# Separate buffers for the last results of W2, and a written order for VectorE and ScalarE, in a float32 chain of attention and two feed-forward layers

## The chip, the cores and the metric

The kernel runs on one core of a Trainium2 chip. Its time is the device time of one execution: 863.34 us is the median of three runs (862.12 to 864.36). One more execution was recorded by the profiler; it took 863.14 us, and its recorded span, from the first to the last instruction, is 861.4 us. Times inside the trace count from the start of that span. PE is TensorE, DVE VectorE, ACT ScalarE, POOL GpSimd, and SP SyncE, which issues most DMAs.

## The reference

```python
# attention: 4 x 8 heads, 768 positions in chunks of 32, window 16 + 32 + 8, 8 memory keys
scores = scale * matmul(q_c, k_full.T); a = softmax(scores); out[c] = matmul(a, v_full)
x = out.transpose(0, 2, 1, 3).reshape(3072, 512)
# first layer, d_ff 1024
h = x @ w_in;  solu = h * softmax(h)
ln = (solu - mean(solu)) / sqrt(var(solu) + 1e-6) * g_ln
x = ln @ w_out
# second layer, d_ff 2048
h = x @ w_in2; g = maximum(0.01 * h, h); out = g @ w_out2
```

Weights come as float64 and are decoded on the chip; everything is computed to float32 accuracy.

## The kernel before, in words

W1, W2, W3 and W4 are the four weight matrices. A float32 product is made from two halves of each operand, a high half (a rounded copy, made by ACT) and a low half (the rest, made by DVE with a subtraction), and three matmuls: high by high, high by low, low by high. A "split" below is one such ACT copy and one such DVE subtraction.

*First stage.* 24 tiles of 128 tokens go through attention, W1, the softmax-like function and the normalization (`s_h`, line 274), a transposition (`s_lt`, 305), and W2 (`s_o`, 343). W2's result for one block of 512 tokens and one quarter `ec` of the 512 features is one accumulator `x2p` of 128 x 512; it takes 24 matmuls, three for each of 8 slices of 128. Two accumulators of PSUM take turns. Each finished one is copied by ACT to the buffer `x2s` (line 356) and stored to `x2d` in HBM by a DMA that ACT issues (line 357). `x2s` has one buffer (`bufs=1`), so a copy must wait until the store of the copy before it has landed. There are 24 such results; the last four, those of block 5, are computed in a loop of their own after the last token tile (line 555).

*Second stage.* W3 is applied to `x2` in a scheme with 7 products instead of 8 on 2 x 2 blocks (P1 to P7). Its operands are sums of quarters of `x2`: `x_steps` (line 504) forms four sums on DVE (lines 510, 512, 516, 526) and splits seven operands (`split`, lines 506 to 508: ACT line 507, DVE line 508), one `yield` after each step. The token blocks make three sets: blocks 0 and 1 (`xs0`, from tile `xt` into the tiles `xP1` to `xP7`), blocks 2 and 3 (`xs1`, from `xtq` into `L2`, `L3` and `xm`), and blocks 4 and 5 (later, into `xP1` to `xP7` again). W3's weights come in pieces, here `L0` and `L1`; `w3_steps` (line 542) splits one in two parts. A unit is one piece of weights by one set of tokens: 7 products of six matmuls each into three accumulators A, B and C (`w3_product`). Units 0 and 1 use `L0` with sets 0 and 1, units 2 and 3 use `L1`, and so on up to 24 units. Within a unit the products P1, P5, P6, P2 and P7 run first, P4 and P3 run during the next unit. After P1 the partial sum in C is copied to `s1`, and after P6 to `u2` (`keep`, line 682); the next product into C must wait for that copy.

*Order.* In the first stage a scheduler orders each engine. From line 535 SP's order is the written one, and from line 658 that of all engines is. Each slot of a unit ends with one or two background steps (`bg`, line 815): first the rest of `xs1`, then the split of `L1`, then the decoding of W4 (`w4_steps`), whose pieces are needed only after the 16th unit. Each engine executes its own instructions in order; one that waits holds up those behind it.

Of the kernel before, what the change touches and what calls it, by code (L numbers as in the profile page):

```python
# [9 lines left out]
F32 = mybir.dt.float32  # L10
F32R = mybir.dt.float32r
U32 = mybir.dt.uint32
AF = mybir.ActivationFunctionType
# [10 lines left out]
LAG = 5  # L24
# [15 lines left out]
def tile_kernel(  # L40
# [12 lines left out]
    nc = tc.nc  # L53
    P = 128
    NTILE = qt.shape[0]
# [5 lines left out]
    KD = DM // P  # L61
    KF = DFF // P
    KF2 = DFF2 // P
    BT = 512
    NBLK = NT // BT
    TB = BT // P
# [5 lines left out]
    x2d = dram.tile([NBLK, P, KD, BT], F32, name="x2d")  # L72
# [72 lines left out]
    sa, sh, satt, sps, sx2 = (ExitStack() for _ in range(5))  # L145
# [194 lines left out]

    open_x2 = {}

    def s_o(b, ec, lh, ll, part):
        if part == 0:
            open_x2[ec] = ps_x2.tile([P, BT], F32, name="x2p")
        ps = open_x2[ec]
        es = slice(ec * P, (ec + 1) * P)
        for kk in range(4 * part, 4 * part + 4):
            for n, (a, r) in enumerate(((w2h, lh), (w2h, ll), (w2l, lh))):
                nc.tensor.matmul(  # L350
                    ps, a[:, kk, es], r[:, kk],
                    start=(kk == 0 and n == 0), stop=(kk == KF - 1 and n == 2),
                )
        if part == 1:
            s = lp.tile([P, BT], F32, name="x2s", bufs=1)
            nc.scalar.activation(s, ps, AF.Copy)  # L356
            nc.scalar.dma_start(out=x2d[b, :, ec, :], in_=s)

    def att_steps(i, ld):
        sc, nms = s_scores(i, ld[0], ld[1])  # L360
# [21 lines left out]
    for d in LOADS:  # L382
# [3 lines left out]
        n = int(d[1])  # L386
# [17 lines left out]
    ENG = mybir.EngineType  # L404
# [5 lines left out]
    lp = sh.enter_context(tc.tile_pool(name="lp", bufs=2, reuse_waits="tile"))  # L410
    lb = {}
# [20 lines left out]
    for i in range(NTILE + 1):  # L432
        a = i + 2
        b, t = divmod(i, TB)
# [4 lines left out]
        if att:  # L439
            p, rs = s_exp(*s_scores(a, ld[0], ld[1]))  # L440
# [13 lines left out]
        if so is not None:  # L454
            j = i - 1
            s_lt(so, j // TB, j % TB, *lb[j // TB])
        so = nso
        if att:
            x = s_pv(pt, ld[2], rs)
# [6 lines left out]
        if 0 <= i - W3_FROM < KF2:  # L466
            f = i - W3_FROM
# [18 lines left out]
    PROD = ("P1", "P5", "P6", "P2", "P7", "P3", "P4")  # L486
# [5 lines left out]
    regr = sr.enter_context(tc.tile_pool(name="regr", bufs=1, side="right", reuse_waits="tile"))  # L492
    reg = {n: regr.tile([P, 4096], F32R, name=n) for n in ("L0", "L1")}
    xrp = sxr.enter_context(tc.tile_pool(name="xrp", bufs=1, side="right", reuse_waits="tile"))
    xr = {r: xrp.tile([P, 2, 2, BT], F32R, name=f"x{r}") for r in PROD}
    xtp = sxt.enter_context(tc.tile_pool(name="xtp", bufs=1, side="right", reuse_waits="tile"))

    def load_xt(v, tb):
# [5 lines left out]
    def x_steps(t, x):  # L504

        def split(r, src):
            nc.scalar.activation(x[r][:, 0], src, AF.Copy)
            tt(out=x[r][:, 1], in0=src, in1=x[r][:, 0].bitcast(F32), op=ALU.subtract)

        tt(out=t["b12"], in0=t["b22"], in1=t["b12"], op=ALU.subtract)  # L510
        yield
        tt(out=t["t2"], in0=t["b12"], in1=t["b11"], op=ALU.add)
        yield
        split("P1", t["b11"])
        yield
        tt(out=t["b11"], in0=t["b22"], in1=t["t2"], op=ALU.subtract)
        yield
        split("P5", t["b11"])
        yield
        split("P6", t["t2"])  # L520
        yield
        split("P2", t["b21"])
        yield
        split("P7", t["b12"])
        yield
        tt(out=t["b12"], in0=t["b21"], in1=t["t2"], op=ALU.subtract)
        yield
        split("P4", t["b12"])
        yield
        split("P3", t["b22"])  # L530
        yield

    ENGS = {ENG.PE, ENG.DVE, ENG.Activation, ENG.Pool, ENG.SP}
    order_ctx = ExitStack()
    order_ctx.enter_context(tc.manual_schedule(engines={ENG.SP}))
    def load_w3(q, n):
        nc.sync.dma_start(
            out=reg[n][:, 1792:3584].bitcast(F32), in_=w3f[q].rearrange("p r f -> p (r f)")
# [3 lines left out]
    def w3_steps(slot):  # L542
        for a, b in ((0, 1024), (1024, 1792)):
            h, l = slot[:, a:b], slot[:, 1792 + a : 1792 + b]
            nc.scalar.activation(h, l.bitcast(F32), AF.Copy)
            tt(out=l, in0=l.bitcast(F32), in1=h.bitcast(F32), op=ALU.subtract)
            yield

    def run(steps):
        for _ in steps:  # L550
            pass

    w3l = [load_w3(q, f"L{q}") for q in range(2)]
    xs0 = x_steps(load_xt(0, xtp.tile([P, 10, BT], F32, name="xt")), xr)
    for i in range(NTILE + 1, NTILE + LAG):
        j = i - LAG
        s_o(j // TB, j % TB, *lb[j // TB], 0)
        s_o(j // TB, j % TB, *lb[j // TB], 1)
    sx2.close()
    sh.close()  # L560
    sa.close()
    regl = sl.enter_context(tc.tile_pool(name="regl", bufs=1, reuse_waits="tile"))
# [11 lines left out]
    }  # L574

    xs1 = x_steps(load_xt(1, xtq), xl_)
    for _ in range(5):
        next(xs0)
    run(w3_steps(w3l[0]))
    run(xs0)  # L580
    for _ in range(3):
        next(xs1)
    sxt.close()
    X = [xr, xl_, xr]
    g3 = sg.enter_context(tc.tile_pool(name="g3", bufs=2, side="right", reuse_waits="tile"))
    dec2 = sd.enter_context(tc.tile_pool(name="dec2", bufs=2, reuse_waits="tile"))

    def load_w4raw(f):
        n = 2 * (f % 3)
# [71 lines left out]
    NA = 2 * NPAIR  # L661
# [56 lines left out]
    def bg(k=1):  # L718
        while k:
            k -= 1  # L720
            while urgent:
                if next(urgent[0], 0) is None:
                    break
                urgent.pop(0)
            else:
                next(w4s, None)
# [41 lines left out]
    for n, (q, v) in enumerate(units):  # L768
# [12 lines left out]
        for j in (0, 1, 2, 3, 4, 6, 5) if n == len(units) - 1 else range(7):  # L781
# [25 lines left out]
            elif j == 5:  # L807
# [4 lines left out]
                    urgent.append(x_steps(xt2, xr))  # L812
                if k >= 4 and k < 7:
                    load_g(k - 4)
            bg(2 if n == 0 or j in (1, 2) and n < NA - 3 else 1)
        older, old = old, u
    for r in ("P4", "P3"):
        w3_product(old, r)
# [145 lines left out]
```

## Time and profile before

| | |
|---|---|
| median of 3 runs | 863.34 us (862.12 to 864.36) |
| the profiled execution | 863.14 us |
| its span | 861.4 us, 1.74 us less than its time |
| granted clock of TensorE, mean | 0.994 |
| PE busy | 825.6 us (96%) |
| DVE busy | 643.6 us (75%) |
| ACT busy | 472.3 us (55%) |

In the page's 40 slices PE is at 9 tenths from the fourth slice to the last but for one, the nineteenth (about 388 to 409 us), where it is at 6; there the granted clock is also at 7 tenths while it is at 9 in all others. That slice holds the passage from W2 to W3, and the change lies there. A granted clock of 1.00 is 2.4 GHz and 0.50 is 1.2 GHz. In a timeline, "idle before" is the time for which the engine did nothing before the instruction, with the instruction that ended it; "x6" says that six instructions are drawn together. Successive matmuls overlap, so the pitch between starts is what counts, not the duration of one.

### The profile page before, as it was taken

How to read it: one execution, taken by the hardware profiler on the slowest of the kernel's cores; microseconds unless marked ns; L12 is line 12 of the kernel's file. 1: busy time of each engine (PE TensorE's matmuls, PEld its weight loads, DVE VectorE, ACT ScalarE, POOL GpSimd, SP SyncE). 2: the span in 40 equal slices, each digit the busy share in tenths (PEclk: the TensorE clock that was granted, in tenths of full speed). 3: DMA queues.
4: the chain of work that ended last, by engine and by line, in shares of the span. 5: the costliest groups of instructions: out<-in, count | busy, mean ns of one | idle time of the engine just before them, and what ended most of it. 6: DMA issues, size and time to landing. Idle time of an engine off the chain costs nothing.

```text
span 861.4 us, 13637 instructions
## 1 busy us (share of the span) xinstructions
PE 825.6 (96%) x4960; PEld 657.3 (76%) x4960; DVE 643.6 (75%) x1145; ACT 472.3 (55%) x1067; POOL 56.4 (7%) x63
## 2 busy tenths in 40 slices
PE   4799999999999999996999999999999999999998
PEld 3467777777777778774888888788777888888886
DVE  6899987677887877768888834756679869668773
ACT  5487854464646454455566545777648445444541
POOL 3333310000000000000000000000000010010001
PEclk9999999999999999997999999999999999999999
DMA  9455576776777655562888756486687476647642
GB/s 327 151 175 193 196 256 202 246 231 220 235 259 245 220 203 175 192 232 84 302 309 310 295 189 232 168 308 265 261 334 245 142 246 200 201 148 238 189 147 98
DMA packets 69891, 190.95 MB, mean 222 GB/s; under 512 B 8000, under 2 KB 32064, under 8 KB 65856
## 3 DMA queue, kind: packets, MB, share of 16 engines
q1 hardware_dynamic: 56864, 175.14, 58.2%
q10 hardware_dynamic: 12960, 14.95, 5.5%
q8 instruction: 39, 0.64, 0.3%
q14 instruction: 28, 0.23, 0.1%
HBM read 129.24 MB, written 60.82 MB: 221 GB/s over the span
## 4 chain that ended last, share of the span: by engine, by line
PE 75%; DVE 13%; ACT 4%; DMA 4%; issue 2%; POOL 1%; ACTq 0%; DVEq 0%; POOLq 0%
PE C L653 24%; PE B L653 13%; PE x2p L350 12%; PE h L91 10%; PE A L653 10%; PE att L203 2%; PE att L245 2%; DMA x2d<-x2s 1%; DMA ring<-gd 1%; DVE so L289 1%; DMA kbd<-in_kw 1%; PE tr L233 1%; DVE m L124 1%; ACT p L220 1%; PE tr L259 1%
## 5 line engine op out<-in xcount | busy, mean ns | idle before, releaser
L350 PE MATMUL x2p<-lhl,w2h 128*128 128x512 f32 x384 | 127.3, 406 | 0.5 <-ACT x2s L356 0.5
L653 PE MATMUL C<-xP,L 128*128 128x512 f32 x384 | 97.1, 395 | 6.9 <-ACT u L682 5.9
L653 PEld LDWEIGHTS C<-xP,L 128*128 128x128 f32 x384 | 72.5, 190 | 24.0 <-ACT u L682 6.7
L350 PEld LDWEIGHTS x2p<-lhl,w2h 128*128 128x128 f32 x384 | 70.1, 189 | 16.6 <-issue 2.0
L350 PE MATMUL x2p<-lhl,w2l 128*128 128x512 f32 x192 | 77.5, 404 | 0.0
L220 ACT ACTIVATE p<-att,nms 128x64 f32<-128x64 f32 x192 | 57.4, 325 | 24.2 <-DVE nms L213 24.1
L91 PE MATMUL h<-w1h,xh 128*128 128x512 f32 x168 | 68.2, 406 | 1.6 <-ACT w1h L133 1.5
L91 PE MATMUL h<-w1l,xh 128*128 128x512 f32 x168 | 66.9, 398 | 2.4 <-POOL w1l L134 2.3
L653 PE MATMUL C<-h,L 128*128 128x512 f32 x192 | 67.0, 390 | 0.1
L91 PE MATMUL h<-w1h,xl 128*128 128x512 f32 x168 | 66.3, 395 | 0.4 <-DVE xl L265 0.4
L764 DVE TENSOR_TENSOR ring<-ring,h 128x512 fp32r<-128x512 f32 x96 | 61.9, 687 | 3.6 <-ACT h L763 2.9
L294 ACT ACTIVATE e<-so,nmu 128x1024 f32<-128x1024 f32 x24 | 27.7, 1153 | 57.7 <-DVE nmu L292 57.2
L679 ACT ACTIVATE g<-g 128x512 f32<-128x512 f32 x72 | 45.0, 626 | 25.6 <-DVE g L698 20.5
L763 ACT ACTIVATE h<-ring 128x512 fp32r<-128x512 f32 x72 | 39.8, 621 | 32.0 <-PE B L653 15.4
L653 PE MATMUL B<-xP,L 128*128 128x512 f32 x192 | 50.3, 398 | 0.2 <-DVE g L708 0.2
L698 DVE TENSOR_TENSOR g<-B,u 128x512 f32<-128x512 f32 x23 | 15.9, 691 | 41.9 <-PE B L653 41.9
L763 ACT ACTIVATE h<-t2k 128x512 fp32r<-128x512 f32 x48 | 28.6, 627 | 31.4 <-DVE t2k L756 18.2
L653 PEld LDWEIGHTS B<-xP,L 128*128 128x128 f32 x192 | 36.6, 191 | 8.6 <-DVE g L708 0.6
L653 PEld LDWEIGHTS C<-h,L 128*128 128x128 f32 x192 | 36.0, 188 | 8.0 <-DVE u L878 0.5
L350 PEld LDWEIGHTS x2p<-lhl,w2l 128*128 128x128 f32 x192 | 36.2, 189 | 7.6 <-issue 1.0
L220 ACT ACTIVATION_READ_ACCUMULATOR p<-att,nms 128x1 f32 x192 | 41.0, 214 | 0.0
L91 PEld LDWEIGHTS h<-w1h,xh 128*128 128x128 f32 x168 | 31.5, 188 | 11.6 <-issue 3.2
(183 smaller groups left out, 1907.3 us busy)
## 6 DMA issues: line engine op xcount, KB each, us to landing
ring<-gd SPq DMA_DIRECT2D x48, 768.0 KB, 4.2
gd<-g SPq DMA_DIRECT2D x24, 1024.0 KB, 5.2
raw<-in_w SPq DMA_DIRECT2D x32, 512.0 KB, 5.3
L<-w3f SPq DMA_DIRECT2D x14, 896.0 KB, 4.8
kbd<-in_kw SPq DMA_DIRECT2D x46, 256.0 KB, 4.3
vbd<-in_vw SPq DMA_DIRECT2D x46, 256.0 KB, 3.7
lnd<-sl SPq DMA_DIRECT2D x16, 512.0 KB, 3.3
lt<-lnd ACTq DMA_DIRECT2D x64, 128.0 KB, 2.8
```

Of the source, the lines that this page charges most:

```text
L91: nc.tensor.matmul(ps, a, b, start=(i == 0), stop=(i == 3 * n - 1))
L124: nc.vector.scalar_tensor_tensor(out=mu, in0=raw[:, :, 1], scalar=0x80000000, in1=mu, op0=ALU.bitwise_and, op1=ALU.bitwise_or,)
L203: nc.tensor.matmul(sc[cs, 2 * hp : 2 * hp + 2, :], q[:, hp, cs], k[:, :, hp, c, :], start=True, stop=True,)
L220: nc.scalar.activation(p[:, h // 2, :, h % 2], sc[:, h], AF.Exp, bias=nms[:, h : h + 1], scale=SCALE, accum_out=rs[:, h : h + 1],)
L245: nc.tensor.matmul(xp[cs, 2 * hp : 2 * hp + 2, :], pt[:, hp, cs], v[:, :, hp, c, :], start=True, stop=True,)
L294: nc.scalar.activation(e, so, AF.Square, bias=nmu, accum_out=ve)
L350: nc.tensor.matmul(ps, a[:, kk, es], r[:, kk], start=(kk == 0 and n == 0), stop=(kk == KF - 1 and n == 2),)
L653: nc.tensor.matmul(acc, w[i], x[j], start=first and n == 0, stop=last and n == 2, skip_group_check=True)
L679: nc.scalar.activation(u.g[:, i], u.g[:, i] if src is None else src, AF.Prelu, alpha=0.01)
L698: tt(out=o.g[:, 1], in0=o.acc["B"], in1=o.u2, op=ALU.add)
L763: nc.scalar.activation(h[:, i], src[n_], AF.Copy)
L764: tt(out=l[:, i], in0=src[n_], in1=h[:, i].bitcast(F32), op=ALU.subtract)
```

## The change

W2's last loop gets a list of destinations. The first two results of block 5 go to two quarters of a new tile `x2t`, which takes the place of `xP4` until that is needed; the third goes to `x2s` as before; the fourth is copied later (`put_x2`), into the first buffer of the pool `dec2`, after the first three steps of `xs1`. The order of DVE and ACT is the written one from this loop on, not only SP's. Written into the loop are the split of `L0` after the first result and 2, 4 and 4 steps of `xs0` after the first, second and third. In `x_steps` the split of P6 now comes between the sum for P5 and P5's split, and the split of P3 between the sum for P4 and P4's split. In units 0 and 1 the slots have one background step each (before: two in all slots of unit 0 and in two slots of unit 1).

```diff
-    def s_o(b, ec, lh, ll, part):
+    def s_o(b, ec, lh, ll, part, s=None):
...
-        if part == 1:
-            s = lp.tile([P, BT], F32, name="x2s", bufs=1)
-            nc.scalar.activation(s, ps, AF.Copy)
-            nc.scalar.dma_start(out=x2d[b, :, ec, :], in_=s)
+        if part == 1 and s != 0:
+            put_x2(b, ec, lp.tile([P, BT], F32, name="x2s", bufs=1) if s is None else s)
+
+    def put_x2(b, ec, s):
+        nc.scalar.activation(s, open_x2[ec], AF.Copy)
+        nc.scalar.dma_start(out=x2d[b, :, ec, :], in_=s)
...
-    xr = {r: xrp.tile([P, 2, 2, BT], F32R, name=f"x{r}") for r in PROD}
+    xr = {r: xrp.tile([P, 2, 2, BT], F32R, name=f"x{r}") for r in PROD if r != "P4"}
+    x2t = xrp.tile([P, 4, BT], F32, name="xP4")
...
         tt(out=t["b11"], in0=t["b22"], in1=t["t2"], op=ALU.subtract)
         yield
+        split("P6", t["t2"])
+        yield
         split("P5", t["b11"])
         yield
-        split("P6", t["t2"])
-        yield
...
         tt(out=t["b12"], in0=t["b21"], in1=t["t2"], op=ALU.subtract)
         yield
+        split("P3", t["b22"])
+        yield
         split("P4", t["b12"])
-        yield
-        split("P3", t["b22"])
         yield
...
-    order_ctx.enter_context(tc.manual_schedule(engines={ENG.SP}))
+    order_ctx.enter_context(tc.manual_schedule(engines={ENG.SP, ENG.DVE, ENG.Activation}))
...
-    for i in range(NTILE + 1, NTILE + LAG):
-        j = i - LAG
+    for n, (j, s) in enumerate(zip(range(NTILE + 1 - LAG, NTILE), (x2t[:, 0], x2t[:, 1], None, 0))):
         s_o(j // TB, j % TB, *lb[j // TB], 0)
-        s_o(j // TB, j % TB, *lb[j // TB], 1)
-    sx2.close()
+        s_o(j // TB, j % TB, *lb[j // TB], 1, s)
+        if n == 0:
+            run(w3_steps(w3l[0]))
+        for _ in range((2, 4, 4, 0)[n]):
+            next(xs0)
+    xr["P4"] = xrp.tile([P, 2, 2, BT], F32R, name="xP4")
+    run(xs0)
...
     xs1 = x_steps(load_xt(1, xtq), xl_)
-    for _ in range(5):
-        next(xs0)
-    run(w3_steps(w3l[0]))
-    run(xs0)
     for _ in range(3):
         next(xs1)
...
+    put_x2(NBLK - 1, KD - 1, dec2.tile([P, 7, 256], F32, name="mm")[:, :2].rearrange("p a c -> p (a c)"))
+    sx2.close()
...
-            bg(2 if n == 0 or j in (1, 2) and n < NA - 3 else 1)
+            bg(2 if j in (1, 2) and 1 < n < NA - 3 else 1)
```

What this does to the order is shown at three places. A number behind a name is the tile's; "waits" names the engines or DMA semaphores an instruction waits for.

ScalarE in W2's last loop, before: the copies to `x2s` (L356), their stores (L357) and the splits of `xs0` (L507).

```order
L356 ACTIVATE x2s_4228<-x2p_4203 128x512 [waits DMAHW5_49,PE_49]
L357 DMA x2d_60<-x2s_4228 128x512 [waits DMAHW1_49,Activation_49]
L507 ACTIVATE xP3_4189<-xt_4198 128x1024 [waits DMAHW0_49]
L507 ACTIVATE xP7_4188<-xt_4198 128x1024 [waits DVE_49]
L356 ACTIVATE x2s_4256<-x2p_4231 128x512 [waits DMAHW1_49,PE_49]
L507 ACTIVATE xP1_4184<-xt_4198 128x1024 [waits DMAHW2_49]
L357 DMA x2d_60<-x2s_4256 128x512 [waits DMAHW4_49,Activation_49]
L507 ACTIVATE xP6_4186<-xt_4198 128x1024 [waits DVE_49]
L507 ACTIVATE xP2_4187<-xt_4198 128x1024 [waits DMAHW6_49,DMAHW3_49]
L356 ACTIVATE x2s_4284<-x2p_4259 128x512 [waits DMAHW4_49,PE_49]
L357 DMA x2d_60<-x2s_4284 128x512 [waits Activation_49]
L507 ACTIVATE xP5_4185<-xt_4198 128x1024 [waits DVE_49]
```

ScalarE there, after (L358 is the copy of a result, L359 its store, L548 the split of `L0`, L510 that of an operand):

```order
L358 ACTIVATE xP4_4190<-x2p_4203 128x512 [waits DVE_49,PE_49]
L359 DMA x2d_60<-xP4_4190 128x512 [waits DMAHW2_49,Activation_49]
L548 ACTIVATE L0_4179<-L0_4179 128x1024 [waits DMAHW7_49]
L548 ACTIVATE L0_4179<-L0_4179 128x768
L358 ACTIVATE xP4_4190<-x2p_4236 128x512 [waits PE_49]
L359 DMA x2d_60<-xP4_4190 128x512 [waits DMAHW4_49,Activation_49]
L510 ACTIVATE xP1_4184<-xt_4198 128x1024 [waits DMAHW1_49]
L510 ACTIVATE xP6_4186<-xt_4198 128x1024 [waits DVE_49]
L510 ACTIVATE xP5_4185<-xt_4198 128x1024 [waits DVE_49]
L358 ACTIVATE x2s_4295<-x2p_4270 128x512 [waits DMAHW6_49,PE_49]
L359 DMA x2d_60<-x2s_4295 128x512 [waits DMAHW5_49,Activation_49]
L510 ACTIVATE xP2_4187<-xt_4198 128x1024 [waits DMAHW3_49]
```

The scheduler's mixture is gone: the first two copies have a buffer each and no wait for a store, the split of `L0` stands behind the first copy (before, it stood earlier, ahead of the last token tile's normalization), and `xP1` is the first operand, not `xP3`.

ScalarE at the start of the second stage, before, from the copy of C to `s1` on:

```order
L682 ACTIVATE s1_4373<-C_4371 128x512 [waits DVE_49,PE_49]
L507 ACTIVATE L2_4321<-xtq_4326 128x1024 [waits DMAHW1_49]
L507 ACTIVATE L2_4321<-xtq_4326 128x1024 [waits DVE_49]
L507 ACTIVATE L3_4322<-xtq_4326 128x1024
L507 ACTIVATE L3_4322<-xtq_4326 128x1024 [waits DMAHW2_49]
L507 ACTIVATE xm2_4328<-xtq_4326 128x1024
L682 ACTIVATE u2_4374<-C_4371 128x512 [waits PE_49]
L507 ACTIVATE xm1_4327<-xtq_4326 128x1024 [waits DVE_49]
```

ScalarE there, after:

```order
L687 ACTIVATE s1_4372<-C_4370 128x512 [waits DVE_49,PE_49]
L510 ACTIVATE L2_4338<-xtq_4343 128x1024 [waits DMAHW0_49]
L358 ACTIVATE mm_4361<-x2p_4305 128x512
L510 ACTIVATE L3_4339<-xtq_4343 128x1024 [waits DVE_49]
L359 DMA x2d_60<-mm_4361 128x512 [waits Activation_49]
L510 ACTIVATE L2_4338<-xtq_4343 128x1024 [waits DVE_49]
L687 ACTIVATE u2_4373<-C_4370 128x512 [waits PE_49]
L510 ACTIVATE L3_4339<-xtq_4343 128x1024 [waits DMAHW1_49]
```

The copy to `u2` (L682, now L687) had five splits of `xs1` ahead of it after `s1`, and has three and the copy of W2's last result now.

VectorE from its first sum of `xs0` on, before (L510, L512, L516 and L526 are the sums, L508 the low halves):

```order
L510 TENSOR_TENSOR xt_4198<-xt_4198 128x1024 [waits DMAHW4_49,DMAHW2_49,DMAHW7_49,DMAHW0_49,DVE_49]
L508 TENSOR_TENSOR xP3_4189<-xt_4198,xP3_4189 128x1024 [waits Activation_49]
L512 TENSOR_TENSOR xt_4198<-xt_4198 128x1024 [waits DMAHW2_49,DVE_49]
L508 TENSOR_TENSOR xP7_4188<-xt_4198,xP7_4188 128x1024 [waits Activation_49]
L508 TENSOR_TENSOR xP1_4184<-xt_4198,xP1_4184 128x1024 [waits Activation_49]
L508 TENSOR_TENSOR xP6_4186<-xt_4198,xP6_4186 128x1024 [waits Activation_49]
L516 TENSOR_TENSOR xt_4198<-xt_4198 128x1024 [waits DVE_49]
L508 TENSOR_TENSOR xP2_4187<-xt_4198,xP2_4187 128x1024 [waits DMAHW6_49,DMAHW3_49,Activation_49]
L526 TENSOR_TENSOR xt_4198<-xt_4198 128x1024
L508 TENSOR_TENSOR xP5_4185<-xt_4198,xP5_4185 128x1024 [waits Activation_49]
L508 TENSOR_TENSOR xP4_4190<-xt_4198,xP4_4190 128x1024 [waits Activation_49]
```

VectorE there, after, from the split of `L0` on (L549; the sums are L513, L515, L519 and L529, the low halves L511):

```order
L549 TENSOR_TENSOR L0_4179<-L0_4179 128x1024 [waits DMAHW7_49,Activation_49]
L549 TENSOR_TENSOR L0_4179<-L0_4179 128x768 [waits Activation_49]
L513 TENSOR_TENSOR xt_4198<-xt_4198 128x1024 [waits DMAHW4_49,DMAHW2_49,DMAHW7_49,DMAHW0_49,DVE_49]
L515 TENSOR_TENSOR xt_4198<-xt_4198 128x1024 [waits DMAHW1_49,DVE_49]
L511 TENSOR_TENSOR xP1_4184<-xt_4198,xP1_4184 128x1024 [waits Activation_49]
L519 TENSOR_TENSOR xt_4198<-xt_4198 128x1024 [waits DVE_49]
L511 TENSOR_TENSOR xP6_4186<-xt_4198,xP6_4186 128x1024 [waits Activation_49]
L511 TENSOR_TENSOR xP5_4185<-xt_4198,xP5_4185 128x1024 [waits Activation_49]
L511 TENSOR_TENSOR xP2_4187<-xt_4198,xP2_4187 128x1024 [waits DMAHW5_49,DMAHW3_49,Activation_49]
L511 TENSOR_TENSOR xP7_4188<-xt_4198,xP7_4188 128x1024 [waits Activation_49]
L529 TENSOR_TENSOR xt_4198<-xt_4198 128x1024 [waits DVE_49]
L511 TENSOR_TENSOR xP3_4189<-xt_4198,xP3_4189 128x1024 [waits Activation_49]
```

The split of `L0` now stands directly ahead of the sums; before, it stood among the decoding of the last piece of W3. The low half of P6 now follows the sum for P5, and the sum for P4 is followed by the low half of P3.

## Rows read from the trace of the kernel before

**Rows 1.** The profile's page, busy time of the engines.

```profile
PE 825.6 (96%) x4960; PEld 657.3 (76%) x4960; DVE 643.6 (75%) x1145; ACT 472.3 (55%) x1067; POOL 56.4 (7%) x63
```

**Rows 2.** Who TensorE waited for from 340 us on (engine, line, releaser).

```profile
PE C L653 <- ACT u L682: 5.9, 2, 5.5
```

**Rows 3.** TensorE's timeline: start us, us, line, operation, idle before and releaser.

```profile
11.11 1.57 PE L233 MATMUL tr<-ident,p 128*128 128x128 f32 x3 [2.15 <-ACT p L220]
...
359.24 1.06 PE L312 MATMUL tr<-ident,so 128*128 128x128 f32 x8 [0.31 <-DVE so L302]
...
361.54 0.73 PE L350 MATMUL x2p<-lhl,w2h 128*128 128x512 f32 x2 [0.48 <-ACT x2s L356]
...
383.19 1.52 PE L653 MATMUL C<-xP,L 128*128 128x512 f32 x6
...
386.63 1.65 PE L653 MATMUL C<-xP,L 128*128 128x512 f32 x6 [0.39 <-ACT s L682]
388.12 1.52 PE L653 MATMUL A<-xP,L 128*128 128x512 f32 x6
395.13 2.93 PE L653 MATMUL C<-xP,L 128*128 128x512 f32 x6 [5.50 <-ACT u L682]
...
405.52 1.74 PE L653 MATMUL C<-L,L 128*128 128x512 f32 x6 [1.91 <-ACT s L682]
...
411.35 1.52 PE L653 MATMUL C<-xm,L 128*128 128x512 f32 x6
412.71 1.52 PE L653 MATMUL C<-xP,L 128*128 128x512 f32 x6
```

**Rows 4.** Windows: length, busy us of PE, PEld, DVE, ACT, POOL; clock, DMA share, GB/s.

```profile
10.00:11.00 1.00, 0.00 (x0) 0.00 (x0) 0.97 (x4) 0.73 (x5) 0.00 (x0) 1.00 0.99 391
395.00:398.00 3.00, 2.87 (x7) 2.29 (x8) 2.65 (x3) 0.36 (x2) 0.00 (x0) 0.50 0.32 124
407.00:410.00 3.00, 3.00 (x8) 2.31 (x7) 2.65 (x6) 0.64 (x2) 0.00 (x0) 0.50 0.49 173
497.00:507.00 10.00, 10.00 (x45) 8.26 (x44) 3.59 (x5) 5.49 (x10) 0.00 (x0) 1.00 0.65 244
```

**Rows 5.** ScalarE's timeline, from the first split of L0 to u2.

```profile
351.96 1.80 ACT L545 ACTIVATE L<-L 128x1024 fp32r<-128x1024 f32 x2 [0.54 <-DMA L<-w3f]
...
367.29 0.60 ACT L356 ACTIVATE x2s<-x2p 128x512 f32<-128x512 f32 x1 [5.81 <-PE x2p L350]
...
371.19 1.06 ACT L507 ACTIVATE xP<-xt 128x1024 fp32r<-128x1024 f32 x1 [0.26 <-DVE xt L510]
374.76 0.60 ACT L356 ACTIVATE x2s<-x2p 128x512 f32<-128x512 f32 x1 [2.51 <-DMA x2d<-x2s]
...
381.43 0.60 ACT L356 ACTIVATE x2s<-x2p 128x512 f32<-128x512 f32 x1 [3.23 <-DMA x2d<-x2s]
...
385.98 0.60 ACT L682 ACTIVATE s<-C 128x512 f32<-128x512 f32 x1 [0.89 <-DVE xP L508]
...
390.71 2.95 ACT L507 ACTIVATE L<-xtq 128x1024 fp32r<-128x1024 f32 x3 [3.18 <-DVE xtq L516]
...
394.51 0.57 ACT L682 ACTIVATE u<-C 128x512 f32<-128x512 f32 x1
```

**Rows 6.** VectorE's timeline in the same stretch.

```profile
358.28 0.81 DVE L302 TENSOR_SCALAR so<-so,nmu,rstd 128x1024 f32<-128x1024 f32 x1 [0.44 <-POOL rstd L297]
...
369.93 1.23 DVE L510 TENSOR_TENSOR xt<-xt 128x1024 f32<-128x1024 f32 x1 [7.45 <-DMA xt<-x2d]
...
383.52 2.36 DVE L508 TENSOR_TENSOR xP<-xt,xP 128x1024 fp32r<-128x1024 f32 x2 [1.42 <-ACT xP L507]
...
401.08 2.09 DVE L546 TENSOR_TENSOR L<-L 128x1024 fp32r<-128x1024 f32 x2
```

**Rows 7.** The instructions on tile x2s: how long its stores took to land.

```profile
DMA to landing us min/median/max: 2.3/4.0/6.8
```

**Rows 8.** The page's list of DMA issues.

```profile
L<-w3f SPq DMA_DIRECT2D x14, 896.0 KB, 4.8
```

## The prediction

> **What bounds the kernel now.** I read the page first: PE is busy for 825.6 of 861.4 us [rows 1], so whatever is gained must come out of the remaining gaps or out of PE's slow time. The list of waits says where the gaps are: from 340 us on the copy to `u2` holds PE for 5.9 us, 5.5 of it once [rows 2]. PE's timeline gives the place. Unit 0 starts at 383.19 and unit 2 at 412.71, that is 29.52 us for twelve products. One product at full pitch is 1.36 us (411.35 to 412.71), so twelve are 16.32, and 13.2 us are lost [rows 3]. Of these 7.8 are waits (5.50 for `u2` at 395.13, 1.91 for `s1` of unit 1 at 405.52, 0.39 for `s1` of unit 0 at 386.63). The other 5.4 is clock and restart: the windows behind both long waits show a granted clock of 0.50, which is 1.2 GHz [rows 4].
>
> What makes `u2` late is read on ACT. Two copies to `x2s` stand idle for the store of the copy before them, 2.51 and 3.23 us [rows 5], and the splits of `xs0` queue behind them; a store takes up to 6.8 us to land here [rows 7]. DVE, which makes the low halves and the sums, starts at 369.93 when `xt` arrives [rows 6]. It finishes the sum for `xs1`'s P5 (L516) just ahead of 390.71, where ACT has waited 3.18 us for it. Then four splits of `xs1` run on ACT before `u2` at 394.51 [rows 5].
>
> **The change part by part.** All times are on the axis of the profiled execution, which took 863.14 us against a median of 863.34, 0.02% less; I sum against 863.14.
>
> *W2's tail.* The split of `L0` leaves the work ahead of the last normalization: 2.09 us of DVE [rows 6] go behind it, some decoding comes ahead of it instead. I estimate that L302 ends 0.3 us earlier (bounds 0 and 1.0, since ACT's normalization pass sits in front too). So the transposes start at 358.94, not 359.24 [rows 3]. The order puts them four matmuls earlier, and these four then cover the copies that PE waited 0.48 for at 361.54 [rows 3]. With 0.82 for the transposes and 1.36 / 6 = 0.227 per matmul, block 5's first result starts at 358.94 + 0.82 + 4 x 0.227 = 360.67, each takes 24 x 0.227 = 5.44, and unit 0 starts at 382.43, 0.76 earlier. Results are ready about 0.2 after their last matmul starts the next group: 366.3, 371.7, 377.2 and 382.6.
>
> *The chain to u2.* ACT copies result 1 at 366.3 to 366.9 without a wait, then splits `L0` (1.80 as in the row at 351.96 [rows 5]) to 368.7, and DVE follows to 370.0. `xt` is there by then: its loads stand on SP behind W3 stores that now come earlier. So DVE's first sum starts at 370.0, practically where it started before, 369.93. From there to the end of the sum for `xs1`'s P5 DVE has 15 operations before and after (11 of `xs0`, then two sums, P1's low half and that sum). Two in a row take 2.36 [rows 6], a pitch of 1.14, so 17.1 us. Before, 3.6 us of waits came on top (369.93 + 17.1 + 3.6 = 390.67, where ACT's row at 390.71 starts). After, I find two waits: 1.2 us for P1's high half, which stands on ACT behind result 2 (371.7 + 0.6 + 1.06 = 373.35, both durations from [rows 5]), and 0.8 for P2's, behind result 3 (377.2). The subtraction put between sum and half fills what were waits of that kind before. That gives 370.0 + 17.1 + 2.05 = 389.2. ACT then needs one split of 1.06 and the copy of 0.57: `u2` is ready at 390.9. Before, three more splits stood in between, 395.1. The copy of result 4 (0.6) falls in ACT's time of waiting for DVE. **Gain here: 395.13 - 390.9 = 4.2 us.** PE arrives at 388.0 and waits 2.9 instead of 5.5.
>
> *Unit 1 and the clock.* Between P7 of unit 0 and unit 2 stand 8 products, 8 x 1.36 = 10.88 us at full pitch. Before they took 412.71 - 395.13 = 17.58: 1.91 wait and 4.8 slow clock and restart. After, with the background steps at one per slot, `s1` of unit 1 has two splits of `xs1`, the copy of C, one `leaky` and one more split ahead of it; with 1.06 and 0.6 each and DVE's low halves at 1.14 I get 397.1 against PE's arrival at 396.3: 0.8 wait, and 0.2 for the next `u2`. **Gain 0.9.**
>
> The clock is the term without a row of its own, since no wait of 2.9 us stands in the trace. It fell behind 5.50 and behind 1.91 us, and stayed at 1.00 around an idle stretch of 2.15 us at 9 to 11 us, as the window there shows [rows 3, 4]. So the bounds are 0 and the 4.8 of before, and the truth can be either. If it falls, one stay at 1.2 GHz like the second of before costs a little over half of the 3 us of the row at 407, 1.7 us; 1.0 of that is swallowed by the two waits just named, which PE then reaches later. I take 0.7 net. **Gain 4.8 - 0.7 = 4.1.**
>
> *What I cost at nothing.* The nine background steps taken out of units 0 and 1 run one unit later, and W4's decoding ends one unit later. DVE has room there: at 497 to 507 it is busy 3.59 of 10 us [rows 4]. Without that cover nine steps of about 0.7 us would cost 6. The reordered splits of the third token set run in the same empty stretch.
>
> **Sum:** 4.2 + 0.9 + 4.1 = 9.2; 863.14 - 9.2 = 853.9 us. From unit 2 on the programs agree, so I carry the gain to the end.
>
> **The rivals.**
>
> *The clock stays low as long as before.* 2.9 us of idleness could cost as much as 5.5 did. For it: the fall behind 1.91 us. Against it: that one came soon after a first fall, and the stretch with 2.15 shows none. With all 4.8 lost and the 1.0 of waits swallowed: 853.9 + (4.8 - 1.0 - 0.7) = 857.0. Beside this, the Trainium skill ("TensorE: Matmul & The Clock Gate", HAM oscillation) says that a burst of matmuls behind an idle gap starts at the halved rate every time the gap re-throttles the array; by that rule the time would lie at 857.0 rather than at the 853.2 of no fall. The trace agrees with it for two gaps and not for the third.
>
> *The waits on stores come back in another place.* `xP4` lies over `x2t`, so its high half on ACT must wait until both stores out of `x2t` have landed. They are issued at 366.9 and 372.3; with 6.8 [rows 7] the second lands at 379.1, and it is needed at 382.3. At twice that landing time, 13.6, it lands at 385.9, 3.6 late, `u2` comes at 394.5, and all but about 1 us of the gain is gone: 862. For it: the stores took 2.3 to 6.8 us in this kernel, and the copy at 374.76 waited for one that ran beside the loads of `xt` and `xtq`. Against it: there are 3.2 us to spare.
>
> *Slower: SP's queue holds up L0.* SP issues in order, and the reload of `L0` for unit 4 stands behind a raw load of W4 which waits for the first decoding; that decoding now begins a unit later. The reload can go when unit 1's P3 has run, about 409.6, lands 4.8 later [rows 8], is split in 2.1 to 3 us, and is needed about 422 (unit 2 at 403.5 plus two units of 9.5). So 5 us are to spare. I place the end of the decoding near 407; from 414.6 on each us of lateness costs one, and from about 424 on the kernel is slower than before: at 426, 865. For it: the order on SP; against it: the raw loads' buffers come free at 391 and 400.
>
> **How the numbers follow.** The forecast, with a clock loss of 0 to 1.7 before swallowing, 852 to 855: 0.65. Clock as low as before, 855 to 858: 0.18. Stores in the way, or another wait of the fixed order of that size, 858 to 863: 0.12. SP's queue: 0.03, and 0.02 for anything else that is slower. The bounds of the unknown parts (chain 1.4 earlier, no waits in unit 1, no fall: 851.5; clock as before and 0.8 of W2's tail not gained: 857.8) make the range 851.5 to 857.8. About 0.3% (2.6 us) is what a measurement of this kernel can tell from no change; faster by more than that has 0.65 + 0.18 and 0.07 of the third case, 0.90; within it 0.05; slower 0.05.
>
> **What would show it.** ACT's copies of block 5 show no idle time for `x2d<-x2s`. `u2` of unit 0 starts near 390.3 and PE waits some 3 us for it. Unit 2's first product starts at 402 to 405 instead of 412.71, and everything behind it is shifted by the same amount. The windows around 391 to 396 settle the clock. The sum is wrong if PE's wait for `u2` is over 4.5 or under 1.5 us, if the clock is at 0.50 for more than 4 us, or if PE shows new waits behind unit 2.

## Result and the profile after

The changed kernel takes 853.36 us (median of 6 runs, 852.24 to 855.21) against 863.69 of before in the same runs: a ratio of 0.9883, 95% interval 0.9867 to 0.9898. The forecast was 853.9 with a range of 851.5 to 857.8. The profiled execution took 853.02 us, 10.12 less than that of before.

Who TensorE waited for from 340 us on, after: total in us, number of waits, longest (answers to [rows 2]):

```profile
PE C L658 <- ACT u L687: 2.6, 1, 2.6
PE C L658 <- ACT s L687: 1.1, 2, 0.8
PE tr L312 <- DVE so L302: 0.6, 1, 0.6
PE C L658 <- ACT g L687: 0.5, 1, 0.5
PE B L658 <- DVE L L549: 0.4, 1, 0.4
...
```

TensorE's timeline after (start, us, line, operation, idle before; answers to [rows 3]):

```profile
358.46 1.06 PE L312 MATMUL tr<-ident,so 128*128 128x128 f32 x8 [0.59 <-DVE so L302]
...
382.28 1.52 PE L658 MATMUL C<-xP,L 128*128 128x512 f32 x6
...
385.98 1.66 PE L658 MATMUL C<-xP,L 128*128 128x512 f32 x6 [0.82 <-ACT s L687]
...
391.66 1.65 PE L658 MATMUL C<-xP,L 128*128 128x512 f32 x6 [2.64 <-ACT u L687]
...
397.70 1.65 PE L658 MATMUL C<-L,L 128*128 128x512 f32 x6 [0.31 <-ACT s L687]
...
403.31 1.53 PE L658 MATMUL C<-xP,L 128*128 128x512 f32 x6
```

Unit 0 starts at 382.28 and unit 2 at 403.31: 21.03 us for the twelve products, where before had 29.52 [rows 3]. This distance, "U0 to U2" below, is the measure of the experiments, since it leaves out what varies ahead of unit 0 (its start lay between 381.97 and 383.93 in the fourteen profiles). It is one execution of each kernel, and it isn't free of chance: the third copy to `x2s` waited 3.23 us for its store in the kernel before and 4.03 in warm2, whose code is the same up to there. From unit 2 to the end it took 447.89 us, before 448.69; over the fourteen profiles this was 447.08 to 449.39, so these 0.8 us are no effect of the change that can be told.

The windows of the stretch after (length, busy us of PE, PEld, DVE, ACT, POOL, granted clock, DMA; answers to [rows 4]):

```profile
388.00:391.00 3.00, 1.02 (x5) 0.51 (x3) 2.97 (x3) 1.66 (x2) 0.00 (x0) 1.00 0.23 87
391.00:396.00 5.00, 4.34 (x19) 3.61 (x20) 4.79 (x6) 3.41 (x6) 0.00 (x0) 1.00 0.31 103
396.00:403.00 7.00, 6.69 (x30) 5.12 (x29) 6.28 (x8) 5.76 (x9) 0.00 (x0) 1.00 0.23 78
```

PE is idle for two thirds of the first window, and the granted clock is 1.00 in all three: it never fell in this stretch of the profiled execution. Of the other five executions only the mean clock of the whole span is recorded (0.993 to 0.998, here 0.996), not where it fell.

ScalarE after (answers to [rows 5]):

```profile
366.16 0.60 ACT L358 ACTIVATE xP<-x2p 128x512 f32<-128x512 f32 x1 [4.85 <-PE x2p L350]
366.79 0.33 ACTq L359 DMA_DIRECT2D x2d<-xP  x1
367.16 1.80 ACT L548 ACTIVATE L<-L 128x1024 fp32r<-128x1024 f32 x2 [0.40 <-ACT xP L358]
371.60 0.60 ACT L358 ACTIVATE xP<-x2p 128x512 f32<-128x512 f32 x1 [2.64 <-PE x2p L350]
...
385.33 0.60 ACT L687 ACTIVATE s<-C 128x512 f32<-128x512 f32 x1 [1.35 <-DVE xP L511]
...
390.06 1.06 ACT L510 ACTIVATE L<-xtq 128x1024 fp32r<-128x1024 f32 x1 [1.34 <-DVE xtq L519]
391.03 0.58 ACT L687 ACTIVATE u<-C 128x512 f32<-128x512 f32 x1
...
397.07 0.57 ACT L687 ACTIVATE s<-C 128x512 f32<-128x512 f32 x1
```

The copies of block 5 now wait for PE's result, not for a store (2.51 and 3.23 us before). One split of `xs1` stands ahead of `u2` behind the sum for P5, before there were four. VectorE after (answers to [rows 6]):

```profile
370.27 1.22 DVE L513 TENSOR_TENSOR xt<-xt 128x1024 f32<-128x1024 f32 x1
371.53 1.23 DVE L515 TENSOR_TENSOR xt<-xt 128x1024 f32<-128x1024 f32 x1
373.70 1.23 DVE L511 TENSOR_TENSOR xP<-xt,xP 128x1024 fp32r<-128x1024 f32 x1 [0.95 <-ACT xP L510]
...
379.26 2.36 DVE L511 TENSOR_TENSOR xP<-xt,xP 128x1024 fp32r<-128x1024 f32 x2 [0.72 <-ACT xP L510]
...
388.80 1.23 DVE L519 TENSOR_TENSOR xtq<-xtq 128x1024 f32<-128x1024 f32 x1
```

Its two waits stand where the prediction put them, 0.95 and 0.72 us.

### The profile page after: what moved, and what is told of

It is laid out like the page before. It is cut to its first block, busy times and chain, and to the rows that moved or that the text cites. A ratio compares the mean times of both kernels' runs of the same rounds, so it can differ in the third digit from the quotient of the medians.

```text
span 851.2 us, 13643 instructions
## 1 busy us (share of the span) xinstructions
PE 821.7 (97%) x4960; PEld 656.4 (77%) x4960; DVE 644.1 (76%) x1145; ACT 472.2 (55%) x1067; POOL 56.2 (7%) x63
## 4 chain that ended last, share of the span: by engine, by line
PE 48%; DVE 3%; DMA 2%; ACT 0%; issue 0%; DVEq 0%
PE C L658 24%; PE B L658 14%; PE A L658 10%; DMA ring<-gd 1%; DMA gd<-g 1%; DVE ring L769 1%; DVE L L653 0%; DVE t2k L761 0%; DVE t L763 0%; DVE g L707 0%; DVE xm L511 0%; DVE g L712 0%; DVE L L511 0%; ACT L L510 0%; ACT xm L510 0%
## 5 line engine op out<-in xcount | busy, mean ns | idle before, releaser
L284 ACT ACTIVATE e<-h,hnm 128x1024 f32<-128x1024 f32 x21 | 23.5, 1119 | 31.2 <-DVE hnm L281 26.4
```

Source lines behind the costliest of these rows:

```text
L284: nc.scalar.activation(e, h, AF.Exp, bias=nm, accum_out=rs)
```

## The experiments

Two theories stood at the start. *Queue (Q):* what stands ahead of the copies `u2` (unit 0) and `s1` (unit 1) in ScalarE's queue sets the end, and the moved background steps are a large part of that. *Buffers (B):* the buffers and the written order carry the gain, and moving the background steps costs nothing and brings nothing. Each of the change's four parts was taken out of the changed kernel, and three were put alone into the kernel before. The times are medians, each beside the kernel before on the same chip; since that took 862.00 to 863.69 us, kernels are compared by their ratios. The expectations name times on a before of about 863.3 and an after of 853.4; where a range is judged by the ratio, it is the ratio times 863.3.

| kernel | us | before there | ratio, 95% | U0 to U2 | PE waits for s1 of unit 0, u2, s1 of unit 1 |
|---|---|---|---|---|---|
| before | | | 1 | 29.52 | 0.39, 5.50, 1.91 |
| after | 853.36 | 863.69 | 0.9883 (0.9867 to 0.9898) | 21.03 | 0.82, 2.64, 0.31 |
| no_bg | 856.71 | 862.53 | 0.9933 (0.9921 to 0.9946) | 25.88 | 0.81, 4.55, 1.71 |
| bg_only | 856.94 | 862.53 | 0.9931 (0.9917 to 0.9945) | 22.47 | 0.40, 3.60, 0 |
| no_buf | 856.64 | 862.53 | 0.9933 (0.9919 to 0.9947) | 24.75 | 4.55, 0.24, 0.30 |
| buf_only | 864.57 | 862.61 | 1.0025 (1.0011 to 1.0039) | 30.80 | 3.46, 3.90, 1.93 |
| buf_right | 859.30 | 862.00 | 0.9973 (0.9960 to 0.9985) | 26.06 | 0, 4.49, 1.75 |
| no_sub | 858.32 | 862.61 | 0.9953 (0.9938 to 0.9968) | 24.90 | 2.90, 2.23, 0 |
| sub_only | 857.89 | 862.00 | 0.9955 (0.9940 to 0.9969) | 25.26 | 0.18, 4.51, 1.74 |
| sched | 851.47 | 862.53 | 0.9869 (0.9855 to 0.9884) | 18.88 | 0, 1.65, 0.26 |
| warm1 | 862.90 | 862.61 | 1.0001 (0.9986 to 1.0015) | 30.43 | 0.39, 0.50, 1.13 |
| warm2 | 863.82 | 862.61 | 1.0010 (0.9994 to 1.0026) | 30.99 | 0.40, 0.52, 0 |
| next | 850.21 | 862.00 | 0.9866 (0.9852 to 0.9880) | 19.10 | 0.82, 0.25, 0 |
| next_sched | 849.67 | 862.00 | 0.9863 (0.9847 to 0.9879) | 16.99 | 0, 0, 0 |

**The background steps.** no_bg is the changed kernel with the old number of steps per slot, bg_only the kernel before with the new one:

```diff
-            bg(2 if j in (1, 2) and 1 < n < NA - 3 else 1)
+            bg(2 if n == 0 or j in (1, 2) and n < NA - 3 else 1)
```

no_bg: 

> The changed kernel with the background steps of before (two per slot in unit 0 and in two slots of unit 1). Theory Q (ScalarE's queue decides: whatever stands ahead of the copies to u2 of unit 0 and s1 of unit 1 delays PE): two more splits ahead of u2, so about 393.6 instead of 391.0; the split of L1, one W4 copy and a wait for g0 ahead of s1 of unit 1, so about 403.4 instead of 397.1; unit 2 at 409 to 411 instead of 403.3 and a time of 859 to 861 us. Theory B (the buffers and the written order carry the gain, moved background steps cost and bring nothing, as the prediction costed them): 853.4 within 0.5 us.

bg_only: 

> The kernel before with one change only: one background step per slot in units 0 and 1. Theory Q: two splits fewer ahead of u2 (393.2 instead of 394.5), no split of L1 and no W4 copy ahead of s1 of unit 1 (about 400 instead of 404.9), unit 2 at 406 to 408 instead of 412.7, a time of 857 to 859 us. Theory B: 863.4 within 0.5 us, since ScalarE still stands idle for two stores.

ScalarE in no_bg, ahead of `u2`:

```profile
390.19 2.00 ACT L510 ACTIVATE L<-xtq 128x1024 fp32r<-128x1024 f32 x2 [1.33 <-DVE xtq L519]
392.10 1.04 ACT L510 ACTIVATE xm<-xtq 128x1024 fp32r<-128x1024 f32 x1
393.05 0.58 ACT L687 ACTIVATE u<-C 128x512 f32<-128x512 f32 x1
```

Up to 390 us this is the changed kernel's order shifted by 0.13. Then two more splits come ahead of `u2`, which starts at 393.05 instead of 391.03; PE waits 4.55 for it, the clock falls (0.50 in the window 394 to 396), and PE waits 1.71 for `s1` of unit 1 as well. In the kernel before, the new number alone gives 0.69% and takes away the whole wait for `s1` of unit 1. The theory of the buffers expected nothing of either, and falls. By the ratios bg_only is 857.3, in the queue theory's range of 857 to 859, and no_bg is 857.5, under its 859 to 861: with buffers and splits in place the steps bring less, and why isn't shown.

**The buffers.** no_buf gives the first two results to `x2s` again; the last one stays in the decoding buffer. buf_only puts all four into `x2t`, in the kernel before. buf_right puts them where the change does, with nothing else of it.

```diff
-    ... (x2t[:, 0], x2t[:, 1], None, 0) ...
+    ... (None, None, None, 0) ...
```

```diff
     # buf_only, in the kernel before
-        s_o(j // TB, j % TB, *lb[j // TB], 1)
+        s_o(j // TB, j % TB, *lb[j // TB], 1, x2t[:, i - NTILE - 1])
```

no_buf: 

> The changed kernel with the first three results of block 5 all through the one buffer x2s; order and steps as changed. Theory Q: the second copy waits for the first store, issued at 366.8, up to 6.8 us, so up to 2 us past 371.6, the third likewise; u2 comes 1 to 3 us later, a time of 854.5 to 857 us. Theory B: most of the 10 us is lost, 859 to 863 us.

buf_only: 

> The kernel before, with block 5's results in buffers of their own (x2t) and nothing else of the change. If the parts' gains add, the buffers bring what taking them out of the changed kernel cost, 3.3 us: 860 to 861. If two chains on ScalarE run beside each other and the later one decides: the copies no longer wait for stores, the sum for xs1's P5 ends near 388.8, three splits (the old background steps) still stand ahead of u2, so u2 comes near 392.3 instead of 394.5, s1 of unit 1 near 402.5 instead of 404.9, and the end at about 403 + 453.2 = 856.2: 855.5 to 857.5, more than half of the whole gain, as the background steps alone gave.

buf_right: 

> The kernel before, with block 5's results where the change puts them (two in x2t, one in x2s, the last in a decoding buffer) and nothing else of the change: ScalarE's and VectorE's orders are left to the scheduler, background steps and splits stay as before. In the first try (the last result in x2t as well) ScalarE waited 2.48 us for that result's store ahead of xP4's half, and the time was 2 us over before. If that place was what hurt: ScalarE no longer waits for stores, the sum for xs1's P5 ends some 2 us earlier (near 388.7), but three splits still stand ahead of u2, and leaky, decoding and L splits ahead of s1 of unit 1; both come 1.5 to 2.5 us earlier and the time falls by as much: 860 to 861.5. If the buffers bring nothing while the old background steps stand in ScalarE's queue: 862.5 to 864. If the parts' gains add: 3.2 us, 859.5 to 860.3.

ScalarE in no_buf (first fence) and in buf_only (second):

```profile
368.02 0.60 ACT L358 ACTIVATE x2s<-x2p 128x512 f32<-128x512 f32 x1 [6.89 <-DMA x2d<-x2s]
...
375.18 0.60 ACT L358 ACTIVATE x2s<-x2p 128x512 f32<-128x512 f32 x1 [4.36 <-DMA x2d<-x2s]
```

```profile
386.06 1.06 ACT L509 ACTIVATE xP<-xt 128x1024 fp32r<-128x1024 f32 x1 [2.48 <-DMA x2d<-xP]
...
388.48 0.60 ACT L685 ACTIVATE s<-C 128x512 f32<-128x512 f32 x1 [1.35 <-DVE xP L510]
```

In no_buf the waits for stores are back, and since the order is written, all behind them is late: PE waits 4.55 for `s1` of unit 0. By the ratio the time is 857.5, 0.5 over the queue theory's 854.5 to 857 and under the 859 to 863 of the buffer theory. In buf_only no copy waits for a store, but the split into `xP4`, which lies over `x2t`, waits 2.48 for the last result's store. That is the prediction's second rival, brought about by my own choice of place: both expectations for that run were wrong in sign. With the last result in the decoding buffer (buf_right) the buffers alone bring 0.27% (2.3 us; the medians differ by 2.7), which both the queue theory (1.5 to 2.5) and adding parts (3.2) can live with: that run clears the buffers of the loss, and tells the two no further apart.

**The order of the splits.** no_sub is the changed kernel, sub_only the kernel before:

```diff
-        split("P6", t["t2"])
-        yield
         split("P5", t["b11"])
         yield
+        split("P6", t["t2"])
+        yield
...
-        split("P3", t["b22"])
-        yield
         split("P4", t["b12"])
         yield
+        split("P3", t["b22"])
+        yield
```

In no_sub the loop also takes one step less of `xs0` behind the third result, since in the old order the split into `xP4` comes one step earlier and has to stay behind the loop.

no_sub: 

> The changed kernel, with the splits of the x sums in their old order (each sum's half directly behind it). The prediction's step: the subtraction fills DVE's waits of that kind, 1.5 us of them; without it u2 comes 1.5 us later: 854.5 to 855.3. With ScalarE's queue counted too: the split of xs1's P6 now stands ahead of u2, one more us, so TensorE waits 3.6 to 5 us for u2, which is where the clock fell in the other runs: 855.5 to 857. If the two orders are worth the same: 853.4 within 0.6.

sub_only: 

> The kernel before, with the new order of the splits alone. Taking it out of the changed kernel cost 5 us, where VectorE then waited 4.9 us instead of 1.7 for high halves. If it adds: 858 to 859. If ScalarE's waits for stores are what makes VectorE wait in the kernel before (2.51 and 3.23 us there), the order can't help before the buffers are there: VectorE saves the 1.13 us ahead of xs1's P5 low half at most, u2 still has three splits ahead, and the time is 861.5 to 863.3.

VectorE in no_sub:

```profile
377.64 2.36 DVE L511 TENSOR_TENSOR xP<-xt,xP 128x1024 fp32r<-128x1024 f32 x2 [1.13 <-ACT xP L510]
...
385.29 2.36 DVE L511 TENSOR_TENSOR xP<-xt,xP 128x1024 fp32r<-128x1024 f32 x2 [1.13 <-ACT xP L510]
...
393.56 3.60 DVE L511 TENSOR_TENSOR L<-xtq,L 128x1024 fp32r<-128x1024 f32 x3 [1.12 <-ACT L L510]
```

A sum with its half directly behind it makes VectorE wait 1.13 us, for ScalarE's copy of 1.06 between them. The wait is there at each of the three sums shown, and at `xs1`'s sums in the kernel before too (1.12 at 391.79 and at 398.81). Without the reordering the changed kernel takes 0.70% more, over all three expectations; the reordering alone brings 0.45%, near the 0.5 to 0.6% of adding parts, where waits for stores as the cause left it at most 0.2%. In sub_only VectorE has no wait left at `xs1`'s sums; at those of `xs0` it still waits 2.07 and 1.35 us for high halves that stand behind copies to `x2s`, and these wait for stores. So waits for stores were not what made VectorE wait at `xs1`'s sums. The profiled execution of sub_only is the fastest of its six (856.56), and `xt` arrives 1.71 us earlier in it than in that of before, so its row in the table flatters it; the 0.45% does not rest on it.

**The written order.** sched is the changed kernel with only SP's order written in the loop:

```diff
-    order_ctx.enter_context(tc.manual_schedule(engines={ENG.SP, ENG.DVE, ENG.Activation}))
+    order_ctx.enter_context(tc.manual_schedule(engines={ENG.SP}))
```

> The changed kernel with only SyncE's order written in W2's last loop; VectorE and ScalarE are ordered by the scheduler again, which takes the splits of xs0 in the sequence P3, P7, P1, P6, P2, P5, P4 and the split of L0 early. Buffers and background steps as changed. Theory Q: u2 and s1 keep the same rows ahead of them, 853.5 to 855.5 us. A rival (the written order itself carries a good part): 857 us or more.

VectorE in sched:

```profile
356.20 0.94 DVE L549 TENSOR_TENSOR L<-L 128x768 fp32r<-128x768 f32 x1
...
370.61 1.22 DVE L513 TENSOR_TENSOR xt<-xt 128x1024 f32<-128x1024 f32 x1 [8.16 <-DMA xt<-x2d]
371.75 1.22 DVE L511 TENSOR_TENSOR xP<-xt,xP 128x1024 fp32r<-128x1024 f32 x1
372.89 1.22 DVE L515 TENSOR_TENSOR xt<-xt 128x1024 f32<-128x1024 f32 x1
374.02 3.49 DVE L511 TENSOR_TENSOR xP<-xt,xP 128x1024 fp32r<-128x1024 f32 x3
```

The scheduler lays a low half between two dependent sums, and VectorE runs on from 370.61 to 385.6 without a stop; the sum for `xs1`'s P5 ends at 388.80, with the written order at 390.03. What the written order does bring is W2's tail: unit 0 starts at 382.28 on average over the five profiles with it (after, no_bg, no_buf, no_sub, next) and at 383.07 over the nine without, though single ones overlap (382.61 in no_sub, 382.09 in sub_only). U0 to U2 is 2.15 us shorter without it, so that unit 2 starts 1.26 earlier in sched than in after. With the copies moved ahead (next and next_sched below) the same edit leaves 0.15 of that, 400.92 against 401.07. By the ratio the time is 852.0, under the queue theory's 853.5 to 855.5. The rival, 857 us or more, falls: the written order carries no good part of the gain. That sched is faster than after isn't shown, since their intervals overlap.

**The clock.** warm1 is the kernel before with 22 extra matmuls between P2 and P7 of unit 0, into a tile that nobody reads; warm2 adds 18 ahead of unit 1's last four products; only the calls are shown.

```diff
     def slot(j, u, o, last):
+        if u.n == 0 and j == 6:
+            warm_pe(22)
+        if u.n == 1 and j == 3:
+            warm_pe(18)      # warm2 alone
```

warm1: 

> The kernel before, with 22 extra matmuls (into a PSUM tile that nobody reads) put on TensorE between the two products that stand around the wait for u2 of unit 0. At the row's pitch of 0.227 us they fill 5.0 of the 5.50 us, so the clock should not fall there. The prediction priced the slow clock behind that wait and the next one as a term that adds to the others: the products from that wait to unit 1's last four took 8.48 us where the changed kernel takes 5.73, so 2.75 us should come back: 860.1 to 861 on a before of 863.3. Rival (ScalarE's queue): the copy to s1 of unit 1 ends at 405.46 whatever TensorE does, so TensorE only waits longer there (1.9 + 2.75 = 4.6 us), the clock falls behind that wait as before, and the time stays within 0.7 us of before: 862.7 to 864.

warm2: 

> As the run with 22 extra matmuls, and 18 more (4.1 us) ahead of unit 1's last four products, so that TensorE is kept busy through both waits. Sum of terms: both falls go, 2.75 + 1.58 (the last four products of unit 1 took 7.19 us before, 5.61 in the changed kernel), so 858.5 to 859.5. ScalarE's queue: only what stands behind the second wait comes back, 1.6 to 2.4 us, so 861 to 862.

TensorE in warm1, ScalarE's copies to `u2` and to `s1` of unit 1 in warm1, that to `s1` before, and the windows of warm2 (length, PE busy, granted clock, DMA):

```profile
395.46 1.65 PE L653 MATMUL C<-xP,L 128*128 128x512 f32 x6 [0.50 <-ACT u L682]
...
402.26 2.47 PE L653 MATMUL C<-xP,L 128*128 128x512 f32 x6 [2.43 <-ACT g L682]
405.85 2.93 PE L653 MATMUL C<-L,L 128*128 128x512 f32 x6 [1.13 <-ACT s L682]
```

```profile
394.83 0.57 ACT L682 ACTIVATE u<-C 128x512 f32<-128x512 f32 x1
...
405.22 0.58 ACT L682 ACTIVATE s<-C 128x512 f32<-128x512 f32 x1
```

```profile
404.88 0.58 ACT L682 ACTIVATE s<-C 128x512 f32<-128x512 f32 x1
```

```profile
388.00:396.00 8.00, 7.86 (x34) 1.00 0.09 18
396.00:404.00 8.00, 5.05 (x21) 1.00 0.31 109
404.00:412.00 8.00, 8.00 (x37) 1.00 0.43 144
412.00:420.00 8.00, 8.00 (x37) 1.00 0.57 213
```

In warm1 PE goes at full clock behind `u2`, reaches the next products sooner, and waits there for ScalarE's copies to `g` (2.43) and `s1` (1.13). Unit 1's last four products start at 405.85 (405.52 before), and the time is where the rival had it, not where the sum of terms had it. From the start of `u2` to that of `s1` of unit 1 ScalarE takes 10.39 us, as before (10.37), though PE's clock is full. So the low clock behind `u2` cost nothing in the kernel before. In warm2 the clock is 1.00 from 388 to 420, and the time is the same as before: both expectations missed. The price of the clock behind the second wait isn't settled by it: the 18 matmuls lasted until 409.04, 2.0 us past the end of `s1`'s copy at 407.01, and ate what they might have brought.

Where no later release is waiting, the low clock does cost. TensorE in bg_only, behind `u2`:

```profile
393.58 2.93 PE L653 MATMUL C<-xP,L 128*128 128x512 f32 x6 [3.60 <-ACT u L682]
396.30 1.64 PE L653 MATMUL C<-L,L 128*128 128x512 f32 x6
...
405.95 1.52 PE L653 MATMUL C<-xP,L 128*128 128x512 f32 x6
```

PE waits for nothing more up to unit 2, and the eight products take 12.37 us instead of 10.88: 1.49 lost, 1.36 of it in the first product (2.72).

**Further ahead in the queue.** next moves `u2` and `s1` of unit 1 ahead in ScalarE's queue (five slots lose their background step, three others get more); next_sched is the same with sched's edit. The main lines of the edit:

```diff
-            bg(2 if j in (1, 2) and 1 < n < NA - 3 else 1)
+            if n == 1 and j == 3:
+                bg(1); leaky(old, 3, old.acc["C"]); bg(1); leaky(old, 2)
+            else:
+                bg({(0,2): 0, (0,4): 0, (0,5): 3, (0,6): 0, (1,0): 2, (1,1): 0, (1,2): 0}.get(
+                    (n, j), 2 if j in (1, 2) and 1 < n < NA - 3 else 1))
...
             keep(u.s1, u.acc["C"])
-            if o is not None:
+            if u.n == 1:
+                leaky(o, 0)
+            elif o is not None:
                 leaky(o, 2)
-        elif j == 2 and o is not None:
+        elif j == 2 and o is not None and u.n != 1:
...
-            leaky(o, 1) if last else leaky(u, 0)
+            if last:
+                leaky(o, 1)
+            elif u.n:
+                leaky(u, 0)
```

next: 

> The changed kernel, with u2 of unit 0 and s1 of unit 1 put further ahead in ScalarE's queue (no background step in four slots of unit 0 and 1, unit 0's first leaky behind s1 of unit 1, the steps made up behind them). If ScalarE's queue is what TensorE still waits for: u2's wait of 2.64 falls below 1, the wait of 0.31 at s1 goes, unit 2 starts near 400.9 instead of 403.3: 850.4 to 851.9 on 853.4. If VectorE's low halves of xs1 decide once u2 is there: TensorE waits for them instead, 852.5 to 853.5.

next_sched: 

> The same as the run before it, with VectorE's and ScalarE's orders in W2's tail left to the scheduler (SyncE's alone written), which gained 1.9 us in the changed kernel. If ScalarE's queue decides there too: u2's wait of 1.65 and the 0.26 at s1 go, 849 to 850.5. If VectorE's low halves decide: 850.8 to 851.5, as that run without the moved copies.

TensorE's waits from 350 to 430 us in next_sched:

```profile
PE x2p L350 <- ACT x2s L358: 0.5, 1, 0.5
PE B L658 <- DVE g L718: 0.4, 1, 0.4
PE tr L312 <- DVE so L302: 0.3, 1, 0.3
```

No wait for `u2` or `s1` is left, and U0 to U2 is 16.99 us; twelve products at the full pitch are 16.32. By their ratios next is 851.7, in its range, and next_sched 851.5, above its 849 to 850.5: the waits bear the queue theory out here, the times don't settle it. next_sched has the lowest time here, 849.67 us and 0.9863 of before (0.9847 to 0.9879), but its interval overlaps those of next, sched and the change.

## Why the prediction was right, and where it was not

*W2's tail:* right in its number. Unit 0 starts at 382.28, forecast 382.43; over all profiles the written order is worth 0.79, forecast 0.76. Two of its parts were off and cancelled: the transposes start at 358.46, not 358.94, and from there to unit 0 it takes 23.82 us, not 23.49.

*The chain to u2:* the place was right, 0.73 us too much was hoped for (3.47 gained, 4.2 forecast). VectorE began at 370.27 instead of 370.0, and waited 1.67 instead of 2.05; but its 15 operations took 18.1 us, not 17.1. I used a pitch of 1.14 for all; an operation on the result just made starts 1.26 us after its predecessor (370.27 and 371.53). The kernel before hid this: what I called 3.6 us of waits there are waits of 1.78 and 1.42, and 0.4 of longer pitch. PE also waited 0.82 for `s1` of unit 0, where the arrival at 388.0 leaves it 0.13: the copy stood 1.35 us for VectorE's last low half of `xs0`. Since `u2` was later still, that cost nothing.

*Unit 1 and the clock:* forecast 0.9 + 4.1, measured 17.58 - (403.31 - 391.66) = 5.93. The wait was 0.31, not 1.0, and the clock didn't fall, where 0.7 was set aside. The time for `s1` was nearly right (ready at 397.64, forecast 397.1). What failed is the name of the larger term: "the clock, gain 4.1". The warm runs show that a full clock behind `u2` brings nothing while `s1` of unit 1 comes from ScalarE at 405.46. From the start of `u2` to that of `s1` ScalarE took 10.37 us before and 6.04 after; these 4.33 are the queue's. The other 1.6 lie in unit 1's last four products, 7.19 us before (405.52 to 412.71) and 5.61 after (397.70 to 403.31). Before, the clock was at 0.50 there and no wait followed, so by the traces this is a price of the clock; no run took it out alone. The Trainium skill ("TensorE: Matmul & The Clock Gate", HAM oscillation) counts the cold matmuls behind each gap as a cost of their own; behind `u2` of the kernel before they ran inside a wait that PE would have had anyway, while the 1.49 us of bg_only agree with it.

*The sum:* 9.2 forecast, 9.40 measured at the start of unit 2 (412.71 - 403.31). That it is this close is luck in part: 0.73 too much in one term and 0.93 too little in the other nearly cancel.

*The background steps at nothing:* right as a cost, since from unit 2 to the end nothing became longer beyond the spread of the profiles; in the 30 us of work where VectorE was least busy (from 502.71 before, 493.31 after) it went from 11.66 us busy to 14.07. The chain to `u2` counts the splits that leave the queue, but nothing in the prediction said that the steps were the largest part alone. Alone, steps, splits and buffers bring 0.69, 0.45 and 0.27%, together 1.41; the three at once (sched) 1.31, and with the written order 1.17. Taken out, they cost 0.50, 0.70 and 0.50, and the written order -0.14, which is inside the intervals. The parts nearly add up, and the written order, which the prediction treated as part of the gain, shows none.

*The rivals:* the wait of `xP4` for a store came in buf_only alone (2.48 us). SP's queue showed no lateness of `L0`: unit 4 starts without a wait, and the new wait of 0.4 us on L549 is in a later unit, at 462.84, where VectorE had stood 1.49 us for a store of `g` ahead of that split. Low clock behind `u2`, the first rival, didn't come in the profiled execution.

## What to carry to other kernels

Where PE waits for a copy, write down everything that stands ahead of that copy and of the next one in the releasing engine's queue; here most of the gain could be read from the order of that queue, not from the length of the gap or the clock behind it. A low clock inside such a stretch costs something only when the next release isn't already later: nothing behind `u2` in the kernel before, 1.49 us in bg_only. Try each part of a change both alone and taken out: here one of four, the written order, brought nothing that could be measured, and the time of the whole change didn't show that.

## What the runs showed of the hardware

The granted clock is not told by the length of one wait: it fell behind waits of 1.91 (before), 2.43 (warm1) and 2.90 us (no_sub), and stayed at 1.00 behind 1.93 (buf_only), 2.43 (warm2) and 2.64 us (after). What ran ahead of the wait differed, and which of it decides stays open.

A store that ScalarE issues takes it 0.33 us, and the next operation starts 0.37 us after the issue (366.79 and 367.16): each of block 5's first three stores holds the next split for that long. The fourth was issued at 387.67 while a split ran, and held nothing. VectorE's pitch of 1.14 us on 128 x 1024 became 1.26 where an operation reads the result of the one ahead of it (370.27 and 371.53) or overwrites what that one reads (373.70 and 374.96: the sum for P5 overwrites P1's operand).
